# Attention scores of four heads on four groups of 32 partitions, in three passes, with one key tile to a step

## The chip, the cores and the metric

The kernel runs on one core of a Trainium2 chip. The metric is the device time of one execution in microseconds (us); times of the engines come from one profiled execution. TensorE (PE in the profile, its weight loads apart as PEld) multiplies into PSUM, which has eight banks of 128 partitions by 512 fp32 values here; ScalarE (ACT) computes the exponentials, VectorE (DVE) and GpSimd (POOL) do the rest of the arithmetic, SyncE (SP) issues the DMAs.

## What is computed

Two layers, each an attention block and a feed-forward block with residuals, on 2048 tokens of width 448. Attention has 16 query heads of width 28 and one shared key and value head.

```python
q = (x @ wq).reshape(B, S, H, Dh).transpose(0, 2, 1, 3)      # H = 16, Dh = 28
k = x @ wk; v = x @ wv
scores = einsum("bhqd,bkd->bhqk", q, k) * (Dh ** -0.5)
p = softmax(scores, axis=-1)
o = einsum("bhqk,bkd->bhqd", p, v)
x = x + o.transpose(0, 2, 1, 3).reshape(B, S, H * Dh) @ wo    # x was layer-normed on the way in
x = x + (silu(x @ w_gate) * (x @ w_up)) @ w_down              # the same
```

Inputs and output are fp32. Products are made of rounded operands: an fp32 value is split into a high part and a low rest (both fp32r), and a product is high·high + high·low + low·high.

## The kernel before, in words

Work runs in phases on one core: the projections of layer 0 (`project`, `q`, L436 to L495), attention of layer 0 (`scores`, L516), its feed-forward block with the projections of layer 1 at its end (`rest`, L814), attention and feed-forward block of layer 1. A schedule written out by hand fixes the order on each engine: what the Python code issues first stands first in that engine's queue, and a queue is worked off in order. A second, slower form of everything (`full=True`, L58) stands behind a branch that these inputs don't take; in the trace there are 2048 score matmuls, which is one pass over both layers.

**Operands of the scores.** `kstack` (`kt_`, L149) holds the transposed keys four times over in 128 partitions: high part in rows 0 to 27, low part in rows 32 to 59, both again in rows 64 to 91 and 96 to 123. `qstack` (`qts`, L151) holds a head's queries in the same rows as high, high, low, low. One matmul that contracts over all 128 partitions thus makes all four products (the low·low one too) in a single pass. Rows 28 and 92 carry a shift of the exponent (the negated rough maximum, in two parts) against a row of ones in `kstack`. Three `qstack` buffers rotate over the 16 groups (`GR`: a block of 512 queries by four heads). `stack` (L340) loads them from DRAM by four DMAs, `high` (L352) loads a second copy of the high parts (`qhigh`), which the rough maximum uses (`quick_steps`, L363): two matmuls against a block-diagonal tile `kdiag`, a maximum on VectorE, and small DMAs that write the rows.

**The attention loop** (L625). For every group `i` and every two key tiles `k2` (128 keys each), `cycle` (L556) makes eight score tiles of 128 keys by 512 queries: four heads by two key tiles. They go into three PSUM pairs of two banks (`pairs`, banks 0 to 5) and into bank 7 (`one`), which is used twice in a cycle, for the first and the last tile. ScalarE takes each pair in one instruction and each single bank in one (`exps`, L549, line L552 in the profile): five instructions, in the order one, pair, pair, one, pair. The first tile of the next cycle has bank 7 free again while ScalarE still works on the last pair. Behind the eight score matmuls stand the products with the values of the cycle before (`pv`, L576): four heads side by side on four groups of 32 columns, accumulated over the 16 key tiles in bank 6. Before the scores of a cycle stands what is slipped in (L561 to L565): the rough maximum (in two cycles of eight), or an output projection (`outproj`, L532, 12 matmuls; 12 times a layer). In group 6 four transposes of the next block's input (`flip`, L244) go in. They borrow the pair that is free at that time. `post` (L587) copies bank 6 out after each group, and normalises it through DRAM.

**The feed-forward block** works with two matmuls of 64 partitions side by side (`side_by_side`, L290, line L295). It needs the upper rows of one input block a second time (`xd`); before, this copy lies in `qstack2` (L748 and L817), which is cleared again for layer 1 (L839).

Of the kernel before, what the change touches and what calls it, by code (L numbers as in the profile page):

```python
# [29 lines left out]
PB = 6  # L30
# [32 lines left out]
def forward(  # L63
# [30 lines left out]
    phase, banks, pairs, live, turn = ExitStack(), [], [], set(), {}  # L94
    LOW, HIGH, ALL = (0, 1, 2, 3), (4, 5, 6, 7), (4, 5, 6, 7, 0, 1, 2, 3)

    def phases():

        n = 0
        while True:  # L100
            for paired in (False, True):
# [3 lines left out]
                if paired:  # L105
                    pairs[:] = [pool.tile([P, 2, 512], F32, name=f"pair{i}") for i in range(3)]
                    banks[:] = [None] * 6 + kept
                else:
                    pairs[:] = []
                    banks[:] = [pool.tile([P, 512], F32, name=f"bank{i}") for i in range(6)] + kept  # L110
                yield
# [194 lines left out]
    class Attention:  # L306
# [33 lines left out]
        def stack(self, i):  # L340
            c, g = GR[i]
            q = qts[i % 3]
            if full:
                for r in (28, 92):
                    dma(q[r : r + 1, :, :], q[r + 1 : r + 2, :, :])
            for b in range(4):
                src = self.qd[c][b // 2, 112 * g : 112 * g + 112, :]
                nc.sync.dma_start(
                    q[32 * b : 32 * b + DH, :, :].bitcast(F32), src.rearrange("(j d) t -> d j t", d=DH)
                )  # L350

        def high(self, i):  # L352

            c, g = GR[i]
            for j in range(4):
                r = 112 * g + DH * j
                nc.sync.dma_start(qms[i % 2][32 * j : 32 * j + DH, :].bitcast(F32), self.qd[c][0, r : r + DH, :])

        def diagonal(self):
            for j in range(4):  # L360
                dma(kd[32 * j : 32 * j + DH, j, :], kt_[0:DH, 0:64])

        def quick_steps(self, i):  # L363
# [4 lines left out]
            def one(t):  # L368
                if t % 2 == 0:
# [3 lines left out]
                    got["pm"][:, 256 * h : 256 * h + 256], qms[i % 2][:, P * t : P * t + P],  # L373
# [11 lines left out]
            def rows():  # L385
                q = qts[i % 3]
                ng = ngs[i % 2]
                two = pers.tile([P, 32], F32R, name="two")
                nc.vector.tensor_copy(two[:, 0:16], ng)
                nc.vector.tensor_tensor(two[:, 16:32], ng, two[:, 0:16], ALU.subtract)  # L390
                flat = pers.tile([P, 32], F32, name="flat")
                nc.vector.transpose(flat, two.bitcast(F32))
                down = pers.tile([P, 32], F32R, name="down")
                nc.vector.tensor_copy(down, flat)
                for b in range(4):
                    to = q[28:93:64, :, :].rearrange("o j (t w) -> o (j t) w", w=P)
                    dma(to[:, :, 32 * b : 32 * b + 32], down[32 * b : 32 * b + 32, :])
# [3 lines left out]
        def max_steps(self, i):  # L401
# [4 lines left out]
            def one(j, qt, kc):  # L406
# [4 lines left out]
                nc.tensor.matmul(pm, q[:, j, P * qt : P * qt + P], kt_[:, ks], start=True, stop=True)  # L411
# [6 lines left out]
            def place(pn=None):  # L418
# [8 lines left out]
                dma(q[28:29, :, :], nh)  # L427
                dma(q[92:93, :, :], nl)
# [7 lines left out]
        def project(self):  # L436
# [14 lines left out]
            if c == 0 and m < 2:  # L451
                if not full:
                    self.waiting.append(lambda: self.high(m))
                self.waiting.append(lambda: self.stack(m))
# [5 lines left out]
        def q(self, c, m):  # L460
# [23 lines left out]
            for z in range(2):  # L484
                for r in (32 * z, 64 + 32 * z):
                    dma(kt_[r : r + DH, cs], two[96 : 96 + DH, z, :])
# [29 lines left out]
        def scores(self, ff):  # L516
            next(switch)
            with tc.tile_pool(name=f"at{self.layer}", bufs=1) as wp:
# [3 lines left out]
                todo, late, due = [], [], {}  # L522
# [20 lines left out]
                def scores(i, which, sp):  # L543
                    for e, (kt, j) in enumerate(which):
                        nc.tensor.matmul(  # L545
                            sp[:, e, :], kt_[:, P * kt : P * kt + P], qts[i % 3][:, j, :], start=True, stop=True
                        )

                def exps(i, which, sp):  # L549
                    two = len(which) == 2  # L550
                    pt = wp.tile([P, 1 + two, 512], F32, name="pt" if two else "pt1", bufs=PB if two else 4)
                    nc.scalar.activation(pt[:, 0 : len(which), :], sp[:, 0 : len(which), :], AF.Exp, scale=SCALE)  # L552
                    for e, w in enumerate(which):
                        pts[i, w] = pt[:, e, :]

                def cycle(i, k2):  # L556


                    a, b, c = (pairs[(8 * i + k2 + n) % 3] for n in range(3))
                    one = banks[7][:, None, :]  # L560
                    self.lent = a[:, 0, :]  # L561
                    if todo and k2 in (0, 5, 6, 7):
                        todo.pop(0)(a[:, 0, :])
                    if full or k2 in (3, 4):
                        self.advance(2 * KC if full else 2)  # L565
                    ks = [(2 * k2 + n // 4, n % 4) for n in range(8)]
# [7 lines left out]
                    return b  # L574

                def pv(i, kt):  # L576
                    if kt == 0:
                        accs[i] = banks[6]
                    for j in range(4):
                        nc.tensor.matmul(  # L580
                            accs[i][32 * j : 32 * j + 32, :], vsb[:, kt, :], pts.pop((i, (kt, j))),
                            start=(kt == 0), stop=(kt == NT - 1), skip_group_check=True,
                        )
                    if kt == NT - 1:
                        due[8 * i + 9] = post(i)
# [39 lines left out]
                for i in range(len(GR)):  # L625
                    for k2 in range(NT // 2):
                        if k2 == 2 and i + 2 < len(GR):
                            self.stack(i + 2)
                        if k2 == 5 and i + 2 < len(GR) and not full:
                            self.high(i + 2)  # L630
                        if i in (2, 3) and k2 == 4:
                            load_wo(i - 2)
                        if k2 == 4 and 10 < i <= 11 + FG:
                            ff.W[i - 11] = weights(i - 11)

                        free = cycle(i, k2)
                        if k2 == 5 and i + 1 < len(GR) and full:
                            self.places[i + 1](free[:, 0, :])
                        if i == 6 and 0 < k2 < 5:
                            flip(got, X0, [k2 - 1], free[:, 0, :])  # L640
                        while late:
                            pv(*late.pop(0))
                        late += [(i, 2 * k2), (i, 2 * k2 + 1)]
                        if 8 * i + k2 in due:
                            due.pop(8 * i + k2)()
                        if i in (5, 9, 14) and k2 > 2:
                            for f in {5: fs, 9: fs1, 14: ff.second[0][:5]}[i][2 * k2 - 6 : 2 * k2 - 4]:
                                f()
                while late:
                    pv(*late.pop(0))  # L650
# [15 lines left out]
    class FeedForward:  # L666
# [147 lines left out]
        def rest(self, xb):  # L814
            self.xbp = xb.enter_context(tc.tile_pool(name=f"xb{self.layer + 1}", bufs=3))
            self.stage = xb.enter_context(tc.tile_pool(name=f"stage{self.layer}", bufs=2))
            dma(qts[2][64:128, 0, :], self.X[0][0][0:64, 3, :])  # L817
            self.X[0] = (*self.X[0][:2], qts[2][:, 0, :])
# [19 lines left out]
            if self.nxt:  # L838
                nc.gpsimd.memset(qts[2].bitcast(F32), 0.0)  # L839
# [21 lines left out]
    nc.gpsimd.memset(kt_.bitcast(F32), 0.0)  # L861
    ones = halves("ones")[0:1, 0, 0:P]
    nc.gpsimd.memset(ones.bitcast(F32), 1.0)
    for r in (28, 92):
        dma(kt_[r : r + 1, :].rearrange("p (a b) -> p a b", b=P), ones[:, None, :].to_broadcast([1, NT, P]))
    nc.gpsimd.memset(vsb, 0.0)
    nc.gpsimd.memset(vsb[:, :, DH : DH + 1], 1.0)
    for t in [*qms, *([kd] if kd is not None else []), *qts]:
# [42 lines left out]
```

## Time and profile before

| | before |
|---|---|
| time, median of 3 runs | 2081.48 us (2077.92 to 2081.76) |
| profiled execution, its time | 2082.3 us |
| its span | 2080.4 us |
| mean granted clock of TensorE | 0.994 |
| VectorE busy | 513.0 us (25%) |
| GpSimd busy | 497.2 us (24%) |
| TensorE weight loads busy | 1445.6 us (69%) |

In the profile's group lines stand line, engine, operation, output and inputs, shapes, the count, then busy time in us and the mean of one in ns, then the idle time before them and what ended it. A timeline line has the start in us from the beginning of the span, the length in us, the engine, line, operation, and how many instructions of the kind were merged into it; a bracket gives the idle time of the engine before it and who ended it. A matmul's length runs to its modelled end, while the next starts earlier: 0.39 us long, but spaced by less.

### The profile page before, as it was taken

Reading aid. Unit: us, or ns where it says so; the run is one execution under the profiler, and the core shown is the slowest. Engines: PE = TensorE matmul, PEld = TensorE weight load, DVE = VectorE, ACT = ScalarE, POOL = GpSimd, SP = SyncE. Lnnn points to the kernel's source line nnn. Section 1 sums busy time; section 2 is a strip of 40 time slices with the busy share of each in tenths; the row PEclk is TensorE's granted clock in tenths of the full one; section 3 lists DMA queues with packets and bytes.
Section 4 is the critical chain, followed back from the end, with each engine's and each line's share of the span. In section 5 each row is a group of like instructions: output and inputs, shape, how many; then the busy total and the mean of one; then the engine's idle time right before and its main releaser. Section 6 shows DMA issues by size and latency. Waiting matters only on the chain.

```text
span 2080.4 us, 36295 instructions
## 1 busy us (share of the span) xinstructions
PE 2042.6 (98%) x14577; PEld 1445.6 (69%) x14577; DVE 513.0 (25%) x1038; ACT 1317.3 (63%) x2382; POOL 497.2 (24%) x499
## 2 busy tenths in 40 slices
PE   6999999999999999999999999999999999999998
PEld 5544544545548999999875445455454589999997
DVE  6111121211104233222550112212111142323322
ACT  2699799798983333333337997988979733333332
POOL 5202011103112333333341111011122023333321
PEclk9999999999999999999999999999999999999999
DMA  6412122123200111000143222121322001111102
GB/s 182 141 40 61 36 50 51 34 51 64 49 7 23 30 30 30 24 22 25 33 116 95 60 51 46 29 56 29 71 43 48 22 8 30 30 30 30 31 2 73
DMA packets 98738, 98.02 MB, mean 47 GB/s; under 512 B 29024, under 2 KB 68352, under 8 KB 98560
## 3 DMA queue, kind: packets, MB, share of 16 engines
q1 hardware_dynamic: 98560, 95.60, 18.7%
q8 instruction: 117, 1.92, 0.4%
q14 instruction: 61, 0.50, 0.1%
HBM read 73.53 MB, written 18.61 MB: 44 GB/s over the span
## 4 chain that ended last, share of the span: by engine, by line
PE 91%; DMA 3%; DVE 2%; SPq 1%; POOL 1%; ACT 1%; issue 0%; DVEq 0%; ACTq 0%; POOLq 0%
PE bank L295 37%; PE bank L580 21%; PE pair L545 16%; PE bank L545 7%; PE bank L273 3%; PE pair L537 3%; DMA o<-rd 2%; PE pair L372 1%; PE bank L537 1%; PE bank L250 1%; DVE stats L219 0%; DMA qd<-q 0%; SPq L595 0%; DVE xn L232 0%; DMA rs<-o 0%
## 5 line engine op out<-in xcount | busy, mean ns | idle before, releaser
L552 ACT ACTIVATE pt<-pair 128x1024 f32<-128x1024 f32 x768 | 764.4, 1030 | 0.8 <-PE pair L545 0.6
L580 PE MATMUL bank<-pt,vsb 128*32 128x512 f32 x4096 | 492.1, 598 | 0.0
L295 PE MATMUL bank<-xh,wgh 64*128 64x512 f32 x1728 | 460.7, 388 | 0.5
L545 PE MATMUL pair<-qstack,kstack 128*128 128x512 f32 x1536 | 399.9, 395 | 0.9 <-ACT q L476 0.9
L295 PE MATMUL bank<-xh,wgl 64*128 64x512 f32 x1404 | 376.1, 386 | 0.0
L552 ACT ACTIVATE pt<-bank 128x512 f32<-128x512 f32 x512 | 308.4, 602 | 90.2 <-PE bank L545 83.8
L295 PE MATMUL bank<-xl,wgh 64*128 64x512 f32 x1296 | 344.1, 387 | 0.0
L295 PE MATMUL bank<-wdh,h 64*128 64x448 f32 x1792 | 339.7, 366 | 1.2 <-ACT h L794 0.8
L545 PEld LDWEIGHTS pair<-qstack,kstack 128*128 128x128 f32 x1536 | 286.6, 188 | 61.7 <-ACT q L476 1.8
L295 PEld LDWEIGHTS bank<-xh,wgh 64*128 64x128 f32 x1728 | 280.2, 184 | 8.5 <-DVE xl L254 1.6
L580 PEld LDWEIGHTS bank<-pt,vsb 128*32 128x32 f32 x4096 | 107.5, 109 | 244.8 <-issue 243.7
L295 PEld LDWEIGHTS bank<-wdh,h 64*128 64x128 f32 x1792 | 256.7, 185 | 8.5 <-issue 2.5
L613 POOL TENSOR_TENSOR o<-o 128x512 f32<-128x512 f32 x32 | 41.1, 1285 | 892.8 <-DMA o<-rd 557.0
L712 POOL TENSOR_TENSOR xres<-stage,xres 128x448 f32<-128x448 f32 x112 | 131.4, 1195 | 488.1 <-ACT stage L711 488.1
L295 PEld LDWEIGHTS bank<-xh,wgl 64*128 64x128 f32 x1404 | 230.0, 184 | 3.7
L302 ACT COPY seen<-bank 128x1 f32<-128x1 f32 x664 | 82.7, 164 | 236.2 <-PE bank L295 234.4
L295 PE MATMUL bank<-wdl,h 64*128 64x448 f32 x896 | 222.5, 360 | 0.0
L545 PE MATMUL bank<-qstack,kstack 128*128 128x512 f32 x512 | 219.0, 428 | 2.7 <-ACT pt L552 2.7
L295 PEld LDWEIGHTS bank<-xl,wgh 64*128 64x128 f32 x1296 | 209.9, 185 | 2.6
L792 ACT ACTIVATE sg<-bank 128x512 f32<-128x512 f32 x112 | 67.1, 599 | 220.1 <-PE bank L295 210.4
L545 PEld LDWEIGHTS bank<-qstack,kstack 128*128 128x128 f32 x512 | 96.1, 188 | 155.9 <-ACT pt L552 144.3
L793 DVE TENSOR_TENSOR sg<-bank,sg 128x512 f32<-128x512 f32 x112 | 77.5, 692 | 491.9 <-ACT sg L792 482.9
(115 smaller groups left out, 1776.3 us busy)
## 6 DMA issues: line engine op xcount, KB each, us to landing
qstack<-qd SPq DMA_DIRECT2D x128, 224.0 KB
qd<-q SPq DMA_DIRECT2D x24, 512.0 KB
o<-rd SPq DMA_DIRECT2D x32, 256.0 KB
qhigh<-qd SPq DMA_DIRECT2D x128, 56.0 KB
wdr<-in_B_w_down_dram SPq DMA_DIRECT2D x28, 224.0 KB
wr<-in_B_w_gate_dram SPq DMA_DIRECT2D x28, 192.0 KB
wr<-in_B_w_up_dram SPq DMA_DIRECT2D x28, 192.0 KB
out_dram<-xres SPq DMA_DIRECT2D x16, 224.0 KB
```

The lines of the kernel that those rows point to most:

```text
L250: nc.tensor.transpose(pt[:, P * t : P * t + P], got["x"][:, t, P * k : P * k + P], ident)
L273: nc.tensor.matmul(po, a, b, start=(i == 0), stop=(i == len(seq) - 1))
L295: nc.tensor.matmul(po, a, b, start=start, stop=stop, skip_group_check=True)
L302: nc.scalar.copy(seen[:, i : i + 1], po[:, 0:1])
L537: nc.tensor.matmul(po[:, 0:D], a[:, g, ts_], b[:, g, :], start=(g + z == 0), stop=(g == NG - 1 and z == 2))
L545: nc.tensor.matmul(sp[:, e, :], kt_[:, P * kt : P * kt + P], qts[i % 3][:, j, :], start=True, stop=True)
L552: nc.scalar.activation(pt[:, 0 : len(which), :], sp[:, 0 : len(which), :], AF.Exp, scale=SCALE)
L580: nc.tensor.matmul(accs[i][32 * j : 32 * j + 32, :], vsb[:, kt, :], pts.pop((i, (kt, j))), start=(kt == 0), stop=(kt == NT - 1), skip_grou ...
L613: nc.gpsimd.tensor_tensor(rb, oraw, rb, ALU.mult)
L712: nc.gpsimd.tensor_tensor(r, s, r, ALU.add)
L792: nc.scalar.activation(sg, pg[0], AF.Silu)
L793: nc.vector.tensor_tensor(sg, pg[1], sg, ALU.mult)
```

## The change

Each of the four heads of a group gets 32 partitions of its own. `keys` holds high and low part of the keys side by side in the free dimension, repeated in four groups of 32 partitions; `qstack` holds head `j` in partitions 32j to 32j+27, high and low part side by side. A score tile is now made in three passes over 32 partitions (high·high, low key·high query, high key·low query), with the weights at `tile_position=(32*j, 0)`, and the four heads' passes stand one behind the other in the queue: pass 0 of heads 0 to 3, pass 1 of heads 0 to 3, pass 2 of heads 0 to 3. Each head has a PSUM bank of its own.

A step is one key tile (512 steps in all) in place of two. Heads 0 to 2 go into a tile of three banks (two such tiles, which take turns), head 3 into bank 7 in every step. ScalarE takes the three banks in one instruction of 128x1536 and bank 7 in a second one, in that order. The products with the values are those of two steps earlier. What is slipped in stands behind the scores of a step and ahead of these products, in the three banks that are free at that time.

Beside it: `qhigh` and `high` go (the rough maximum reads the high part from `qstack`), `stack` keeps four DMAs in another shape, `kdiag` is filled by GpSimd in place of DMAs, `keys` is preset to ones and zeros in place of two DMAs of a row of ones, and the feed-forward block gets tiles `xd` of its own, so that `qstack2` isn't cleared again.

```diff
-    kt_ = pers.tile([P, S], F32R, name="kstack")
+    keys = pers.tile([P, 2, S], F32R, name="keys")
+    kh, kl = keys[:, 0, :], keys[:, 1, :]
-    qts = [pers.tile([P, 4, 512], F32R, name=f"qstack{n}") for n in range(3)]
-    qms = [pers.tile([P, 512], F32R, name=f"qhigh{n}") for n in range(2)] if not full else []
+    qts = [pers.tile([P, 2, 512], F32R, name=f"qstack{n}") for n in range(3)]
...
-                    pairs[:] = [pool.tile([P, 2, 512], F32, name=f"pair{i}") for i in range(3)]
+                    threes[:] = [pool.tile([P, 3, 512], F32, name=f"three{i}") for i in range(2)]
...
         def stack(self, i):
-            for b in range(4):
-                src = self.qd[c][b // 2, 112 * g : 112 * g + 112, :]
-                nc.sync.dma_start(
-                    q[32 * b : 32 * b + DH, :, :].bitcast(F32), src.rearrange("(j d) t -> d j t", d=DH)
-                )
-        def high(self, i):
...
+                nc.sync.dma_start(
+                    q[32 * j : 32 * j + DH, :, :].bitcast(F32),
+                    self.qd[c][:, r : r + DH, :].rearrange("z d t -> d z t"),
+                )
         def diagonal(self):
             for j in range(4):
-                dma(kd[32 * j : 32 * j + DH, j, :], kt_[0:DH, 0:64])
+                nc.gpsimd.tensor_copy(kd[32 * j : 32 * j + DH, j, :], kh[32 * j : 32 * j + DH, 0:64])
...
-                def cycle(i, k2):
-                    a, b, c = (pairs[(8 * i + k2 + n) % 3] for n in range(3))
-                    one = banks[7][:, None, :]
...
-                    for where, which in ((one, ks[0:1]), (b, ks[1:3]), (c, ks[3:5])):
-                        scores(i, which, where)
-                        exps(i, which, where)
-                    scores(i, ks[5:7], a)
-                    scores(i, ks[7:8], one)
-                    exps(i, ks[7:8], one)
-                    exps(i, ks[5:7], a)
+                def step(n):
+                    i, kt = divmod(n, NT)
+                    three, one = threes[n % 2], banks[7]
+                    q, ks = qts[i % 3], slice(P * kt, P * kt + P)
+                    for z, (k, part) in enumerate(((kh, 0), (kl, 0), (kh, 1))):
+                        for j in range(4):
+                            js = slice(32 * j, 32 * j + 32)
+                            nc.tensor.matmul(
+                                three[:, j, :] if j < 3 else one, k[js, ks], q[js, part, :],
+                                start=(z == 0), stop=(z == 2), tile_position=(32 * j, 0),
+                            )
+                    pt = wp.tile([P, 3, 512], F32, name="pt", bufs=4)
+                    pt1 = wp.tile([P, 512], F32, name="pt1", bufs=4)
+                    nc.scalar.activation(pt, three, AF.Exp, scale=SCALE)
+                    nc.scalar.activation(pt1, one, AF.Exp, scale=SCALE)
+                    pts[n] = [*(pt[:, j, :] for j in range(3)), pt1]
+                def between_steps(n):
+                    i, kt = divmod(n, NT)
+                    free = threes[(n + 1) % 2]
+                    self.lent = free[:, 0, :]
+                    if full or kt in (6, 8):
+                        self.advance(KC if full else 2)
...
+                    if todo and kt in (0, 10, 12, 14):
+                        todo.pop(0)(free[:, 1, :])
+                    if i == 6 and kt in (2, 4, 6, 8):
+                        flip(got, X0, [kt // 2 - 1], free[:, 2, :])
...
+                for n in range(last):
+                    i, kt = divmod(n, NT)
+                    if kt == 4 and i + 2 < len(GR):
+                        self.stack(i + 2)
...
+                    step(n)
+                    between_steps(n)
+                    if n > 1:
+                        pv(n - 2)
+                    if n in due:
+                        due.pop(n)()
...
-                self.X[c] = xtile(self.xbp, qts[2][:, c, :])
+                self.X[c] = xtile(self.xbp, self.xd[c])
...
-            if self.nxt:
-                nc.gpsimd.memset(qts[2].bitcast(F32), 0.0)
...
-    nc.gpsimd.memset(kt_.bitcast(F32), 0.0)
+    nc.gpsimd.memset(kh.bitcast(F32), 1.0)
+    nc.gpsimd.memset(kl.bitcast(F32), 0.0)
```

More of the change, by code (lines that the diff above doesn't have):

```diff
@@ L28 @@
 SCALE = DH ** -0.5
-PB = 6
 LEAD = 4
@@ L93, in forward @@
     kept = [ps.tile([P, 512], F32, name=f"bank{n}") for n in (6, 7)]
-    phase, banks, pairs, live, turn = ExitStack(), [], [], set(), {}
+    phase, banks, threes, live, turn = ExitStack(), [], [], set(), {}
     LOW, HIGH, ALL = (0, 1, 2, 3), (4, 5, 6, 7), (4, 5, 6, 7, 0, 1, 2, 3)
@@ L100, in phases @@
         while True:
-            for paired in (False, True):
+            for wide in (False, True):
                 n += 1
@@ L387, in rows @@
                 ng = ngs[i % 2]
-                two = pers.tile([P, 32], F32R, name="two")
-                nc.vector.tensor_copy(two[:, 0:16], ng)
-                nc.vector.tensor_tensor(two[:, 16:32], ng, two[:, 0:16], ALU.subtract)
+                two = pers.tile([P, 4, 2, 4], F32R, name="two")
+                parts, whole = [two[:, :, z, :] for z in range(2)], ng.rearrange("p (j t) -> p j t", t=4)
+                nc.vector.tensor_copy(parts[0], whole)
+                nc.vector.tensor_tensor(parts[1], whole, parts[0], ALU.subtract)
                 flat = pers.tile([P, 32], F32, name="flat")
-                nc.vector.transpose(flat, two.bitcast(F32))
+                nc.vector.transpose(flat, two.rearrange("p j z t -> p (j z t)").bitcast(F32))
                 down = pers.tile([P, 32], F32R, name="down")
@@ L410, in one @@
                 pm, ks = self.mbank()[1], slice(512 * kc, 512 * kc + 512)
-                nc.tensor.matmul(pm, q[:, j, P * qt : P * qt + P], kt_[:, ks], start=True, stop=True)
+                js, qs = slice(32 * j, 32 * j + 32), slice(P * qt, P * qt + P)
+                for n_, (z, k) in enumerate(((0, kh), (1, kh), (0, kl))):
+                    nc.tensor.matmul(
+                        pm, q[js, z, qs], k[js, ks], start=(n_ == 0), stop=(n_ == 2), tile_position=(32 * j, 0)
+                    )
                 nc.vector.tensor_reduce(got["mx"][:, n, kc : kc + 1], pm, AX.X, ALU.max)
@@ L483, in q @@
                 return
-            for z in range(2):
-                for r in (32 * z, 64 + 32 * z):
-                    dma(kt_[r : r + DH, cs], two[96 : 96 + DH, z, :])
+            for j in range(4):
+                dma(keys[32 * j : 32 * j + DH, :, cs], two[96 : 96 + DH, :, :])
             vt = pers.tile([P, 512], F32, name="sg")[64:96, :]
@@ L521, in scores @@
                 on, accs, pts = {}, {}, {}
-                todo, late, due = [], [], {}
+                todo, due = [], {}
                 def load_wo(z):
@@ L541, in outproj @@
                         nc.vector.tensor_tensor(xres[:, 4 * c + t, :], po[:, 0:D], xres[:, 4 * c + t, :], ALU.add)
[L543 to L554, printed above, removed]
@@ L577, in pv @@
+                def pv(n):
+                    i, kt = divmod(n, NT)
                     if kt == 0:
@@ L624, in scores @@
                 ff.second = norm_steps(2)
[L625 to L650, printed above, removed]
+                last = NT * len(GR)
+                for n in range(last):
+                    i, kt = divmod(n, NT)
+                    if kt == 4 and i + 2 < len(GR):
+                        self.stack(i + 2)
+                    if i in (2, 3) and kt == 8:
+                        load_wo(i - 2)
+                    if kt == 8 and 10 < i <= 11 + FG:
+                        ff.W[i - 11] = weights(i - 11)
+                    step(n)
[4 more added lines that the diff above has]
+                        due.pop(n)()
+                    if i in (5, 9, 14) and kt > 5:
+                        for f in {5: fs, 9: fs1, 14: ff.second[0][:5]}[i][kt - 6 : kt - 5]:
+                            f()
+                for n in (last - 2, last - 1):
+                    pv(n)
                 self.lent = None
@@ L815, in rest @@
             self.xbp = xb.enter_context(tc.tile_pool(name=f"xb{self.layer + 1}", bufs=3))
-            self.stage = xb.enter_context(tc.tile_pool(name=f"stage{self.layer}", bufs=2))
-            dma(qts[2][64:128, 0, :], self.X[0][0][0:64, 3, :])
-            self.X[0] = (*self.X[0][:2], qts[2][:, 0, :])
+            self.stage = xb.enter_context(tc.tile_pool(name=f"stage{self.layer}", bufs=1 if full else 2))
+            xd = xb.enter_context(tc.tile_pool(name=f"xd{self.layer}", bufs=1))
+            self.xd = [xd.tile([P, 512], F32R, name=f"xd{c}") for c in range(NC)]
+            dma(self.xd[0][64:128, :], self.X[0][0][0:64, 3, :])
+            self.X[0] = (*self.X[0][:2], self.xd[0])
             self.turned(1)
@@ L860, in forward @@
     at.turned(0)
-    nc.gpsimd.memset(kt_.bitcast(F32), 0.0)
[L862 to L865, printed above, removed]
+    nc.gpsimd.memset(kh.bitcast(F32), 1.0)
+    nc.gpsimd.memset(kl.bitcast(F32), 0.0)
     nc.gpsimd.memset(vsb, 0.0)
     nc.gpsimd.memset(vsb[:, :, DH : DH + 1], 1.0)
-    for t in [*qms, *([kd] if kd is not None else []), *qts]:
+    for t in [*([kd] if kd is not None else []), *qts]:
         nc.gpsimd.memset(t.bitcast(F32), 0.0)
```

37 lines of the change are left out of this document (15 added, 22 removed).

## The prediction

> **What bounds the kernel now.** I read the page's totals and its chain first, then busy times by stretch, then the timeline of one undisturbed cycle.
>
> ```profile
> span 2080.4 us, 36295 instructions
> PE 2042.6 (98%) x14577; PEld 1445.6 (69%) x14577; DVE 513.0 (25%) x1038; ACT 1317.3 (63%) x2382; POOL 497.2 (24%) x499
> PE 91%; DMA 3%; DVE 2%; SPq 1%; POOL 1%; ACT 1%; issue 0%; DVEq 0%; ACTq 0%; POOLq 0%
> ```
>
> ```profile
> 75.98:614.96 538.98, 536.69 (x3265) 269.70 (x3267) 81.78 (x232) 493.53 (x639) 80.28 (x80) 1.00 0.22 48
> 1104.20:1643.79 539.59, 536.89 (x3265) 269.62 (x3267) 82.54 (x232) 493.60 (x639) 80.31 (x80) 1.00 0.22 48
> sum 1078.57, PE 1073.58 PEld 539.32 DVE 164.32 ACT 987.12 POOL 160.59; mean PE 536.79 PEld 269.66 DVE 82.16 ACT 493.56 POOL 80.29
> ```
>
> The two stretches run from the first to the last score matmul of each layer's attention: 1078.6 us, which is all that the change rewrites. TensorE is busy through it and carries the chain, but ScalarE is busy for 987 us of it (92%): two engines stand close together there, and what one waits for the other soon matters.
>
> ```profile
> 404.89 0.50 PE L545 MATMUL bank<-qstack,kstack 128*128 128x512 f32 x1
> 405.22 1.56 PE L545 MATMUL pair<-qstack,kstack 128*128 128x512 f32 x6
> 406.62 0.39 PE L545 MATMUL bank<-qstack,kstack 128*128 128x512 f32 x1
> 406.94 1.92 PE L580 MATMUL bank<-pt,vsb 128*32 128x512 f32 x16
> 408.79 0.50 PE L545 MATMUL bank<-qstack,kstack 128*128 128x512 f32 x1
> ```
>
> ```profile
> 405.94 1.94 ACT L552 ACTIVATE pt<-pair 128x1024 f32<-128x1024 f32 x2
> 407.77 0.61 ACT L552 ACTIVATE pt<-bank 128x512 f32<-128x512 f32 x1
> 408.24 1.05 ACT L552 ACTIVATE pt<-pair 128x1024 f32<-128x1024 f32 x1
> ```
>
> A bare cycle of two key tiles lasts 408.79 − 404.89 = 3.90 us on TensorE. The six matmuls from 405.22 and the seventh at 406.62 are spaced by 0.23; a change between the two shapes of matmul costs some 0.1 more (406.62 to 406.94 is 0.32). The products with the values take 408.79 − 406.94 = 1.85 for two key tiles. ScalarE's pairs are spaced by (407.77 − 405.94) / 2 = 0.915, a single bank by 408.24 − 407.77 = 0.47: 3 × 0.915 + 2 × 0.47 = 3.69 of the 3.90. Of 1078.6 us, 256 × 3.90 = 998 are bare cycles; the other 80 is what is slipped in.
>
> **What the change makes of a step.** By throughput alone it looks good. On ScalarE a step would need the three banks, 0.915 for two of them and for the third what one bank more costs, and the single one at 0.47.
>
> ```profile
> L552 ACT ACTIVATE pt<-pair 128x1024 f32<-128x1024 f32 x768 | 764.4, 1030 | 0.8 <-PE pair L545 0.6
> L552 ACT ACTIVATE pt<-bank 128x512 f32<-128x512 f32 x512 | 308.4, 602 | 90.2 <-PE bank L545 83.8
> ```
>
> A bank more is 1.030 − 0.602 = 0.43, so the three banks take 1.345 until the next instruction starts, and the step 1.345 + 0.47 = 1.81, against 3.69 / 2 = 1.845 before. (The form of 128x1536 isn't in this trace. Three single banks would be 3 × 0.47 = 1.41, one and a half pairs 1.37; I keep 1.345, the row's own slope.)
>
> But the queue has a wait in each step that can't hide. Head 3 has bank 7 alone. Its pass 0 of step n+1 must wait until ScalarE has read bank 7 of step n, and that is the last thing ScalarE does in step n. Behind the waiting matmul in TensorE's queue stand the passes 1 and 2 of all heads, the products with the values and everything later; ScalarE's next instruction, the three banks of step n+1, waits for pass 2 of head 2. So in each step ScalarE stands still while TensorE makes two passes. Before, ScalarE still has a pair queued when bank 7 is asked for; only the very first cycle, without the products in between, shows the same pattern:
>
> ```profile
> 79.41 0.60 ACT L552 ACTIVATE pt<-bank 128x512 f32<-128x512 f32 x1
> ...
> 78.32 0.39 PE L545 MATMUL bank<-qstack,kstack 128*128 128x512 f32 x1
> 80.06 0.50 PE L545 MATMUL bank<-qstack,kstack 128*128 128x512 f32 x1 [1.35 <-ACT pt L552]
> 80.40 1.77 PE L545 MATMUL pair<-qstack,kstack 128*128 128x512 f32 x6
> ...
> 80.06 0.19 PEld L545 LDWEIGHTS bank<-qstack,kstack 128*128 128x128 f32 x1 [1.79 <-ACT pt L552]
> 80.17 0.19 PEld L545 LDWEIGHTS pair<-qstack,kstack 128*128 128x128 f32 x1
> ```
>
> Bank 7 is done at 79.41 + 0.60 = 80.01; the weight load, which carries the wait too, starts at 80.06: 0.05 from ScalarE to TensorE. The matmul is 0.50 long rather than 0.39, as its weights weren't loaded ahead (0.11, the spacing of the loads at 80.06 and 80.17).
>
> What follows a release with several groups of partitions is shown by the feed-forward block, which runs two of 64 side by side; here the upper one waited:
>
> ```profile
> 661.16 0.86 PE L295 MATMUL bank<-xh,wgh 64*128 64x512 f32 x2
> 661.53 0.18 PEld L295 LDWEIGHTS bank<-xh,wgh 64*128 64x128 f32 x1 [0.38 <-DVE sg L793]
> 661.54 0.29 PEld L295 LDWEIGHTS bank<-xl,wgh 64*128 64x128 f32 x2
> 661.54 0.72 PE L295 MATMUL bank<-xl,wgh 64*128 64x512 f32 x2
> 661.64 0.41 PEld L295 LDWEIGHTS bank<-xh,wgl 64*128 64x128 f32 x2
> 661.88 0.40 PE L295 MATMUL bank<-xh,wgl 64*128 64x512 f32 x1
> 662.12 0.60 PE L295 MATMUL bank<-xh,wgh 64*128 64x512 f32 x2
> ```
>
> Three things are to be seen. The lower half's next load (661.54), which waits for nothing of its own, came only with the released one: a blocked head of the queue holds the other groups as well. Loads of the two groups then start within 0.01 of each other, so they overlap. And the next round of matmuls starts at 661.88, 0.34 after the release, the one after at 662.12, 0.24 later. I take the same for four groups of 32: with the release of bank 7, head 3's pass 0 and the others' pass 1 start together; 0.34 later, behind head 3's pass 1, pass 2 of heads 0 to 2; it is 0.40 long (the matmul at 661.88). That is 0.74 from release to the end of pass 2.
>
> (The Trainium skill, TensorE: Matmul & The Clock Gate, Part 3, gives 3.07 times the speed for four row tiles of 32, where four would be perfect; this trace has no four. By it, as an estimate, a round of four would take 4 × 0.23 / 3.07 = 0.30, and as one round lies on the path, the step would be 0.07 longer and the whole 36 us, which the range holds.)
>
> Last, from TensorE to ScalarE:
>
> ```profile
> 405.42 0.60 ACT L552 ACTIVATE pt<-bank 128x512 f32<-128x512 f32 x1
> 405.45 0.40 PE L545 MATMUL pair<-qstack,kstack 128*128 128x512 f32 x1
> ```
>
> The matmul at 404.89 ends at 405.39 and ScalarE starts at 405.42: 0.03. The one at 405.45 completes a pair at 405.85 and its exponential starts at 405.94: 0.09. The new wide instruction carries the same two waits as that pair, so I take 0.10.
>
> The step: 1.345 (three banks) + 0.60 (bank 7, to its end) + 0.05 + 0.74 + 0.10 = **2.84 us**, against 1.95 before. 512 × 2.84 = 1454 us.
>
> TensorE's own work fits inside, which is why its gain is worth nothing: three rounds at 0.34, 0.23 and 0.32 and half of 1.85 for the products, with one more change of shape, 0.05, make 1.87 of 2.84.
>
> **What is slipped in.** The rough maximum (two matmuls, 0.5 us) now falls into this idle second: free. An output projection doesn't fit:
>
> ```profile
> 230.21 0.47 PE L537 MATMUL pair<-woh,onh 128*128 128x448 f32 x1
> ...
> 232.75 0.40 PE L545 MATMUL bank<-qstack,kstack 128*128 128x512 f32 x1
> ...
> 288.49 0.69 DVE L253 CAST xh<-pair 128x512 fp32r<-128x512 f32 x1 [1.87 <-PE pair L250]
> 289.21 0.69 DVE L254 TENSOR_TENSOR xl<-pair,xh 128x512 fp32r<-128x512 f32 x1
> ```
>
> Its 12 matmuls take 232.75 − 230.21 = 2.54. From a release: the third round starts at 0.34 + 0.23 = 0.57, the projection at 0.90, it ends at 3.44, the products (0.1 + 0.93 + 0.05) at 4.5; then all three rounds of the next step follow, one more than after a wait. The step is 4.5 − 2.84 + 0.23 = 1.9 longer, times 24 is 45 us. The eight transposed blocks hold a bank for VectorE's two instructions (0.69 each) and cost some 0.5 each: 5 us with two that meet a rough maximum. First and last step of each layer: 5 us. Attention: 1454 + 45 + 5 + 5 = 1509.
>
> **The rest** I cost at nothing, with ±10 us for it: fewer and shorter DMAs for the queries, one clearing of a buffer less, GpSimd copies for `kdiag`. They stand beside the projections, where TensorE is the bound as the chain has it; DMA is 3% of that chain. If the cover is gone, a query load that comes late costs a few us once a group, but each is issued 28 steps ahead. SyncE's queue holds nothing new in front of it.
>
> **Sum.** The profiled execution took 2082.3 us (span 2080.4), 0.8 above the median of 2081.48. 2082.3 + 1509 − 1078.6 = 2512.7; against the median 2512.
>
> **Rivals.**
>
> *The other heads pass the blocked one (faster).* If TensorE let heads 0 to 2 make their passes while head 3 waits for bank 7, the three banks would be ready when ScalarE ends the step, and the bound would be TensorE's 1.87: 512 × 1.87 + 80 = 1037, a gain of 41 us, **2040**. It decides as soon as pass 2 of head 2 can end ahead of bank 7's release. For it: the groups are independent, and TensorE has a second to spare. Against: rows 661.16 to 661.54, where the free half stood still for 0.37. (The Trainium skill, same page and part, says that weight loads may be pulled ahead for another row group but that matmuls start and end in their order; by that rule this rival falls, and the trace agrees.)
>
> *Weight loads one after the other.* Twelve loads a step rather than four. If four groups don't load at once, eight stand between the release and pass 2 of head 2: the last begins at 7 × 0.11 = 0.77, then 0.11 and 0.40, 1.28 rather than 0.74: 512 × 0.54 = 276, **2790**. Against it: the two loads at 661.53 and 661.54; four are not shown.
>
> *No side by side at all*, the change not doing what it says: eight matmuls behind the release, 0.34 + 6 × 0.23 + 0.40 = 2.12 rather than 0.74: 512 × 1.38 = 707, **3220**. Against it: the same rows, and the four column groups of L580, 16 of which take 1.92.
>
> *A slower clock.* TensorE would idle for about 0.9 us in each step; the granted clock is 1.00 in both stretches now. At half of it 0.74 would be 1.4: some 340 us more, **2850**.
>
> **Chances.** Forecast 0.80, the faster rival 0.05, serial loads 0.06, no overlap 0.05, clock 0.02; 0.02 for smaller gains that I don't see. The forecast's own bounds: 0.03 to 0.10 into ScalarE (−36), three banks at 1.33 to 1.41 (−8 to +33), the round (+36), the rest ±10, projections ±15: 2440 to 2600, which serves as the range, since the other cases hold 2 in 10. Faster by over 0.2% (about what a measurement tells here) 0.06, within it 0.01, slower 0.93.
>
> **What would show it.** In the attention stretches ScalarE's wide instruction should show about 0.9 us idle ahead of it, ended by a score matmul, 500 times, some 450 us in all; TensorE's first load of bank 7 should be ended by ScalarE's single exponential each step; steps spaced by 2.84; the stretches about 1509 us. Wide instructions with no idle time and bank 7 without a wait would make me wrong; rounds spaced by more than 0.4 would name the second or third rival, a clock below 1.00 the last.

## The result, and the profile after

| | before | changed |
|---|---|---|
| median | 2080.28 us (4 runs, 2077.92 to 2081.76) | 2497.32 us (4 runs, 2496.78 to 2499.42) |
| ratio | | 1.2008, 95% interval 1.1987 to 1.2029 |
| span of the profiled execution | 2080.4 us | 2495.9 us |
| attention stretches | 1078.6 us | 1507.8 us |
| outside of them | 1001.8 us | 988.1 us |

The change makes the kernel 20% slower; 2512 us were forecast, 2440 to 2600 as the range. The page of the changed kernel, and the two stretches from the first to the last score matmul of each layer:

```profile
span 2495.9 us, 44645 instructions
PE 2257.7 (90%) x18673; PEld 1392.6 (56%) x18673; DVE 516.6 (21%) x1038; ACT 1315.6 (53%) x2126; POOL 494.2 (20%) x504
PE 60%; issue 22%; ACT 14%; DVE 2%; SPq 1%; DMA 1%; POOL 0%; ACTq 0%; DVEq 0%
...
L552 ACT ACTIVATE pt<-three 128x1536 f32<-128x1536 f32 x512 | 742.6, 1450 | 515.7 <-PE three L546 444.7
L546 PE MATMUL bank<-qstack,keys 32*128 32x512 f32 x1536 | 495.5, 428 | 199.7 <-ACT pt L553 198.5
```

```profile
70.10:824.50 754.40, 649.08 (x5321) 246.34 (x5324) 81.88 (x232) 495.00 (x512) 80.00 (x80) 1.00 0.09 22
1306.40:2059.80 753.40, 649.56 (x5321) 246.54 (x5324) 86.49 (x232) 495.10 (x512) 79.87 (x80) 1.00 0.09 22
sum 1507.80, PE 1298.64 PEld 492.88 DVE 168.38 ACT 990.11 POOL 159.87; mean PE 649.32 PEld 246.44 DVE 84.19 ACT 495.05 POOL 79.94
```

ScalarE does as much as before in attention (990 us busy, 987 before), but in 1508 us instead of 1079: 66% rather than 92%. Ahead of its wide exponential it stood idle for 515.7 us in all, 444.7 of them ended by a score matmul, and the score matmuls into bank 7 waited 198.5 us for `pt L553`, the exponential of bank 7. Each engine waits for the other in turn. That TensorE is "busy" for 90% of the span says little: each matmul counts to its modelled end. The timeline of one step, ScalarE, TensorE, and the weight loads around the release:

```profile
402.21 0.59 ACT L553 ACTIVATE pt<-bank 128x512 f32<-128x512 f32 x1
403.71 1.45 ACT L552 ACTIVATE pt<-three 128x1536 f32<-128x1536 f32 x1 [0.90 <-PE three L546]
405.06 0.59 ACT L553 ACTIVATE pt<-bank 128x512 f32<-128x512 f32 x1
```

```profile
402.86 0.49 PE L546 MATMUL bank<-qstack,keys 32*128 32x512 f32 x1 [0.50 <-ACT pt L553]
402.86 0.50 PE L546 MATMUL three<-qstack,keys 32*128 32x512 f32 x3
403.19 0.39 PE L546 MATMUL bank<-qstack,keys 32*128 32x512 f32 x1
403.20 0.39 PE L546 MATMUL three<-qstack,keys 32*128 32x512 f32 x3
403.43 0.39 PE L546 MATMUL bank<-qstack,keys 32*128 32x512 f32 x1
403.75 1.07 PE L575 MATMUL bank<-pt,vsb 128*32 128x512 f32 x8
404.75 0.51 PE L546 MATMUL three<-qstack,keys 32*128 32x512 f32 x3
405.70 0.50 PE L546 MATMUL bank<-qstack,keys 32*128 32x512 f32 x1 [0.45 <-ACT pt L553]
```

```profile
402.86 0.18 PEld L546 LDWEIGHTS bank<-qstack,keys 32*128 32x128 f32 x1 [0.82 <-ACT pt L553]
402.86 0.19 PEld L546 LDWEIGHTS three<-qstack,keys 32*128 32x128 f32 x3
```

Bank 7 is read until 402.21 + 0.59 = 402.80. At 402.86 head 3's pass 0 starts, and the other three heads' pass 1 with it. At 403.20 the three make pass 2, which ends at 403.59; ScalarE's wide instruction starts at 403.71, after 0.90 us of idling. Pass 0 of the next step's heads 0 to 2 starts at 404.75, long before head 3 gets bank 7 again at 405.70: 2.84 us after the last time.

### The profile page after: what moved, and what is told of

The parts are those of the page before. It is cut to its first block, busy times and chain, and to the rows that moved or that the text cites. A ratio compares the mean times of both kernels' runs of the same rounds, so it can differ in the third digit from the quotient of the medians.

```text
span 2495.9 us, 44645 instructions
## 1 busy us (share of the span) xinstructions
PE 2257.7 (90%) x18673; PEld 1392.6 (56%) x18673; DVE 516.6 (21%) x1038; ACT 1315.6 (53%) x2126; POOL 494.2 (20%) x504
## 4 chain that ended last, share of the span: by engine, by line
PE 60%; issue 22%; ACT 14%; DVE 2%; SPq 1%; DMA 1%; POOL 0%; ACTq 0%; DVEq 0%
PE bank L294 31%; PE bank L546 12%; ACT pt L553 10%; PE three L546 6%; PE bank L575 3%; ACT pt L552 3%; PE three L532 3%; PE bank L272 2%; PE three L365 1%; PE bank L532 1%; PE bank L249 1%; DVE xl L253 0%; SPq L131 0%; DMA qd<-q 0%; DVE stats L218 0%
## 5 line engine op out<-in xcount | busy, mean ns | idle before, releaser
L552 ACT ACTIVATE pt<-three 128x1536 f32<-128x1536 f32 x512 | 742.6, 1450 | 515.7 <-PE three L546 444.7
L546 PE MATMUL bank<-qstack,keys 32*128 32x512 f32 x1536 | 495.5, 428 | 199.7 <-ACT pt L553 198.5
L546 PE MATMUL three<-qstack,keys 32*128 32x512 f32 x4608 | 625.3, 459 | 5.8 <-DVE xl L253 3.4
L575 PE MATMUL bank<-pt,vsb 128*32 128x512 f32 x4096 | 546.8, 606 | 0.0
L546 PEld LDWEIGHTS three<-qstack,keys 32*128 32x128 f32 x4608 | 250.8, 183 | 435.2 <-issue 352.8
L546 PEld LDWEIGHTS bank<-qstack,keys 32*128 32x128 f32 x1536 | 244.8, 184 | 369.6 <-ACT pt L553 350.0
L294 PE MATMUL bank<-xh,wgh 64*128 64x512 f32 x1728 | 427.1, 388 | 0.5
L553 ACT ACTIVATE pt<-bank 128x512 f32<-128x512 f32 x512 | 303.1, 592 | 0.0
L294 PEld LDWEIGHTS bank<-xh,wgh 64*128 64x128 f32 x1728 | 246.4, 184 | 8.6 <-DVE xl L253 1.6
L294 PEld LDWEIGHTS bank<-xl,wgh 64*128 64x128 f32 x1296 | 184.4, 184 | 2.9
L575 PEld LDWEIGHTS bank<-pt,vsb 128*32 128x32 f32 x4096 | 81.3, 108 | 173.2 <-issue 163.3
```

Source lines behind the costliest of these rows:

```text
L294: nc.tensor.matmul(po, a, b, start=start, stop=stop, skip_group_check=True)
L546: nc.tensor.matmul(three[:, j, :] if j < 3 else one, k[js, ks], q[js, part, :], start=(z == 0), stop=(z == 2), tile_position=(32 * j, 0),)
L552: nc.scalar.activation(pt, three, AF.Exp, scale=SCALE)
L553: nc.scalar.activation(pt1, one, AF.Exp, scale=SCALE)
L575: nc.tensor.matmul(accs[i][32 * j : 32 * j + 32, :], vsb[:, kt, :], pts[n][j], start=(kt == 0), stop=(kt == NT - 1), skip_group_check=True,)
```

## Experiments

Theory: head 3's bank is asked for in the middle of TensorE's queue and released as the last thing in ScalarE's, and whatever stands behind the blocked matmul stands still with it. Main rival: twelve small matmuls with twelve weight loads in place of four large ones, with changes of shape in every step, are too much for TensorE. Single profiled runs have no interval of their own. In the swaps and with fewer passes the differences are far above the spread of a few us that the timed kernels show; outside attention they are not, and there the spread is told with them.

### The order on ScalarE alone

```diff
-                    nc.scalar.activation(pt, three, AF.Exp, scale=SCALE)
                     nc.scalar.activation(pt1, one, AF.Exp, scale=SCALE)
+                    nc.scalar.activation(pt, three, AF.Exp, scale=SCALE)
```

> The changed kernel with ScalarE's two exponentials of a step in the other order: bank 7 first, the three banks second. All twelve score matmuls, all weight loads and the order on TensorE stay. Theory (the wait for bank 7, asked for first and released last, costs ScalarE two rounds in every step): bank 7 is free 0.6 us after the scores are done, long before TensorE asks for it, so the step falls from 2.85 us to what TensorE needs by itself, about 1.87 (ScalarE needs 1.81); with some 80 us of slipped-in work per run the attention stretches fall from 1508 to about 1040 us and the kernel to about 2030 (2010 to 2070), faster than the kernel before. Rival (twelve small matmuls and weight loads in place of four, or changes of shape twice as often, are what costs): the order on ScalarE changes nothing, about 2497.

Measured: 2089.65 us (5 runs), 1.0037 times the kernel before (1.0022 to 1.0051). Two swapped lines take away 408 of the 417 us. No matmul was changed, so the rival falls. The wait for bank 7 is gone, 0.3 us where it was 199.7:

```profile
L546 PE MATMUL bank<-qstack,keys 32*128 32x512 f32 x1536 | 491.7, 425 | 0.3 <-ACT pt L552 0.3
```

But it isn't the 2030 that I expected. One bare step on TensorE:

```profile
301.32 0.50 PE L546 MATMUL three<-qstack,keys 32*128 32x512 f32 x3
...
303.22 0.50 PE L546 MATMUL three<-qstack,keys 32*128 32x512 f32 x3
```

The step is 303.22 − 301.32 = 1.90 rather than 1.87, 15 us over 512 (a key tile took 3.90 / 2 = 1.95 before). The rest is slipped-in work: the stretches take 1099.3 us, so 1099.3 − 512 × 1.90 = 126 us of it, where the 80 of the kernel before was expected. A step with a rough maximum shows about half of these 46 us:

```profile
207.74 0.51 PE L546 MATMUL three<-qstack,keys 32*128 32x512 f32 x3
...
208.91 0.51 PE L365 MATMUL three<-kdiag,qstack 128*128 128x256 f32 x2 [0.21 <-ACT pt L553]
209.35 1.06 PE L575 MATMUL bank<-pt,vsb 128*32 128x512 f32 x8
210.34 0.50 PE L546 MATMUL three<-qstack,keys 32*128 32x512 f32 x3
```

It takes 210.34 − 207.74 = 2.60, 0.70 more than a bare step (`L553` is the wide exponential in this kernel). The two matmuls borrow the three banks that ScalarE now reads last, and wait 0.21 for them; they also stand between two other shapes. The kernel before had three pairs, one was free by then, and the same two matmuls (`L372` there) wait for nothing:

```profile
211.15 0.50 PE L545 MATMUL bank<-qstack,kstack 128*128 128x512 f32 x1
...
215.06 0.50 PE L372 MATMUL pair<-kdiag,qhigh 128*128 128x256 f32 x2
...
219.55 0.39 PE L545 MATMUL bank<-qstack,kstack 128*128 128x512 f32 x1
```

Two cycles with a rough maximum last 219.55 − 211.15 = 8.40 there, two bare ones 7.80: 0.30 for each. 60 steps have one, so 60 × 0.40 = 24 us of the 46. By medians over the same two traces an output projection costs 2.93 in place of 2.45 (24 of them, 12 us), and the eight steps with transposes cost 9 us more.

In attention the new layout thus stays 1099.3 − 1078.6 = 20.7 us longer than the old one even with the order swapped. That the whole kernel comes within 0.4% is due to the time outside attention, 988.5 us against 1001.8.

### Fewer passes

The third pass left out (no product of high key and low query), and then the second as well (no product with a low part):

```diff
-                    for z, (k, part) in enumerate(((kh, 0), (kl, 0), (kh, 1))):
+                    for z, (k, part) in enumerate(((kh, 0), (kl, 0))):
...
```

> The changed kernel without the third pass (high key times low query is left out, so its scores lack that product). Theory of the wait: one round fewer lies between the release of bank 7 and the end of the three banks, so the step loses one round, 0.235 us: 2.61 us, about 2375 in all. Rival of TensorE's throughput: 1.9 of the 2.85 us belong to twelve score matmuls, eight cost a third less, so the step loses about 0.6: about 2180.

Measured: 2380.5 us. ScalarE's timeline:

```profile
400.30 1.45 ACT L552 ACTIVATE pt<-three 128x1536 f32<-128x1536 f32 x1 [0.61 <-PE three L546]
...
402.91 1.45 ACT L552 ACTIVATE pt<-three 128x1536 f32<-128x1536 f32 x1 [0.67 <-PE three L546]
```

The step is 2.61 and the idle time 0.67 in place of 0.90: a third of the score matmuls gone, and the step is one round shorter, no more. That is the wait's arithmetic and not that of throughput.

> The changed kernel with the first pass alone (high times high; both products with a low part are left out). Theory of the wait: heads 0 to 2 need no matmul behind the blocked one any more, the three banks are ready before bank 7 is released, and the wait vanishes from ScalarE's path: the step falls to ScalarE's own 1.82 us, a second drop of about 0.8 us after one of 0.235, in all about 1980. Rival of throughput: the second pass left out gives as much as the first, about 0.6 us again or less.

Measured: 2122.57 us, not 1980. The three banks are indeed ready without the blocked matmul, but something is left:

```profile
329.79 1.46 ACT L552 ACTIVATE pt<-three 128x1536 f32<-128x1536 f32 x1
331.14 0.60 ACT L553 ACTIVATE pt<-bank 128x512 f32<-128x512 f32 x1
331.37 0.50 PE L546 MATMUL three<-qstack,keys 32*128 32x512 f32 x3
331.79 0.49 PE L546 MATMUL bank<-qstack,keys 32*128 32x512 f32 x1
331.98 1.45 ACT L552 ACTIVATE pt<-three 128x1536 f32<-128x1536 f32 x1 [0.24 <-PE three L546]
332.21 1.07 PE L575 MATMUL bank<-pt,vsb 128*32 128x512 f32 x8
333.20 0.50 PE L546 MATMUL three<-qstack,keys 32*128 32x512 f32 x3
333.81 1.45 ACT L552 ACTIVATE pt<-three 128x1536 f32<-128x1536 f32 x1
```

Steps are 2.19 and 1.83 in turn. The matmul that waits for bank 7 (331.79, after 331.14 + 0.60) also holds back the products with the values (332.21) and, through them, the next three heads (333.20). I had followed the queue behind the blocked matmul only to the next exponential. The second pass left out gave 2.61 to about 2.0, more than the 0.24 of the first one, as the wait has it and as a cost per matmul has not; its size was 0.2 too large. That is 0.19 × 512 = 97 of the 143 us over 1980; the rest is slipped-in work that costs more than I assumed.

### The same wait in the kernel before

```diff
-                    exps(i, ks[7:8], one)
                     exps(i, ks[5:7], a)
+                    exps(i, ks[7:8], one)
```

> The kernel before, with one swap: in each cycle the last pair is exponentiated ahead of the second use of bank 7, so that bank 7 is released last there too. No passes, no new shapes, all else as before. Theory of the wait: ScalarE loses about 0.7 us in each cycle of two key tiles; a cycle goes from 3.90 to about 4.46 us, 143 us over 256 cycles, less some 30 for slipped-in work that now falls into idle time: 2190 to 2225. Rival (the three passes cost the time, not the order): about 2080 as before.

Measured: 2185.05 us. A cycle on TensorE and ScalarE:

```profile
133.56 0.51 PE L545 MATMUL bank<-qstack,kstack 128*128 128x512 f32 x1 [0.48 <-ACT pt L552]
...
138.02 0.50 PE L545 MATMUL bank<-qstack,kstack 128*128 128x512 f32 x1 [0.48 <-ACT pt L552]
```

```profile
134.62 2.85 ACT L552 ACTIVATE pt<-pair 128x1024 f32<-128x1024 f32 x3
137.35 0.62 ACT L552 ACTIVATE pt<-bank 128x512 f32<-128x512 f32 x1
138.55 0.60 ACT L552 ACTIVATE pt<-bank 128x512 f32<-128x512 f32 x1 [0.58 <-PE bank L545]
```

138.02 − 133.56 = 4.46, as worked out. So some 105 us come from one swapped line with none of the new layout in it. That the total is 5 us under the expected range is mostly the slipped-in work: the two stretches grew by 1184.7 − 1078.6 = 106 us, so 37 us of it, and not 30, fell into the idle time; the time outside attention came out 3 us shorter in this trace. The wait alone is shown, in both kernels and both ways.

### The 13.7 us outside attention

The changed kernel gains 5.9 us ahead of layer 0's scores and 7.3 between the layers' scores, which I had costed at nothing. Five kernels ask where from:

```diff
-                nc.gpsimd.tensor_copy(kd[32 * j : 32 * j + DH, j, :], kh[32 * j : 32 * j + DH, 0:64])
+                dma(kd[32 * j : 32 * j + DH, j, :], kh[0:DH, 0:64])
```

> The changed kernel, but the block-diagonal tile of keys is filled by four DMAs from the first keys again, as in the kernel before, rather than by GpSimd. It asks where the 13.7 us come from that the changed kernel gains outside the attention stretches (5.9 us ahead of the first scores, 7.3 us from the end of layer 0's scores to the start of layer 1's). Theory of the query loads (in the projections SyncE's queue has the four loads of the second query copy less to issue, and the other loads stand one projection earlier, so the stores of the projected queries land sooner and their buffers come free sooner): no difference here, the stretches outside attention stay at 988 us. Rival (the DMAs of the diagonal wait for the keys and hold SyncE's queue): about 6 us of loss in each layer, 1000 us outside attention.

Measured: 2496.7 us, with 988.7 us outside attention (its span of 2494.8 less two stretches that add up to 1506.1). No difference in the sum.

```diff
...
+                if not full:
+                    self.waiting.append(lambda: self.high(m))
                 self.waiting.append(lambda: self.stack(m))
```

> The changed kernel with the loads of the second query copy put back during the projections alone (two groups a layer, four DMAs each, in the old places of the queue, into a scratch buffer in DRAM that nothing reads). Theory of the query loads: the gain outside attention goes, 988 us back to about 1000. Rival of the diagonal: 988 us as it is.

Measured: 2505.05 us. Outside attention, ahead of, between and behind the stretches:

```profile
0.00:73.30 73.30, 55.30 (x244) 42.97 (x244) 39.77 (x81) 20.28 (x35) 38.26 (x67) 0.98 0.64 189
828.60:1313.60 485.00, 479.49 (x4021) 447.65 (x4020) 173.67 (x285) 162.08 (x551) 167.27 (x166) 1.00 0.14 40
2067.40:2503.30 435.90, 426.33 (x3777) 410.35 (x3777) 135.34 (x208) 143.76 (x518) 129.29 (x113) 0.99 0.10 30
```

994.2 us: 3.2 more ahead of the scores (73.3 against 70.1) and 3.1 between them (485.0 against 481.9). How much of that is spread is seen in the other kernels of this document whose projections are those of the changed kernel (the exponentials swapped, two passes, one pass, the diagonal by DMA, the buffer cleared): 68.1 to 69.9 us ahead, 481.8 to 484.3 between, 987.4 to 989.2 in all. The kernel before with its exponentials swapped has 75.1, 486.8 and 998.5, where the kernel before has 76.0, 489.2 and 1001.8. So 5 to 7 us in all come back, of a gain of 10 to 14: about half of it was this load. Ahead of the scores that is clear; between the layers 485.0 lies too near to 484.3 to tell. The remainder was sought in the clearing of the third query buffer:

> The changed kernel with the clearing of the third query buffer between the layers put back on GpSimd (now half the size, about 1 us). The second query copy explained 8 of the 13.7 us gained outside attention, 5 of 6 ahead of layer 0 but 3 of 7 between the layers; this asks whether the clearing holds the other 4 there. If it stands in front of GpSimd's share of the projections: 1 to 4 us more between the layers, 2498 to 2501. If not: 2497, and the rest belongs to the shorter loads (the four loads of a group carry half the bytes).

Measured: 2497.82 us, nothing. (The split of "8 of 13.7" in that text was taken from the totals; by the stretches it is 6.) No part of the rest is seen in the clearing, though the spread between the layers would hide an effect of up to 2 us. From the other side, the kernel before with the load of group 1's queries moved behind the projections:

```diff
-                self.waiting.append(lambda: self.stack(m))
+                if full or m == 0:
+                    self.waiting.append(lambda: self.stack(m))
...
+                        if i == k2 == 0 and not full:
+                            self.stack(1)
```

> The kernel before with one load moved: the queries of group 1 are loaded at the start of the attention loop rather than during the projections (they are needed 16 key tiles later). Theory of the query loads: the 3 us that SyncE spends on them no longer stand ahead of the stores of projected queries, and most of the 6 us a layer comes off: 2080 to about 2070 (2067 to 2075). Rival (the order of SyncE's queue isn't what delays, or the diagonal is): about 2080.

Measured: 2072.97 us, 0.9963 times the kernel before (0.9950 to 0.9977), with 992.0 us outside attention in place of 1001.8. That load's four issues stand in SyncE's queue ahead of the stores of projected queries, in the kernel before (here ahead of layer 1):

```profile
1077.89 3.10 SPq L348 DMA_DIRECT2D qstack<-qd  x4
1081.09 0.38 SPq L479 DMA_DIRECT2D qd<-q  x1
```

and ScalarE waits for those stores before it can fill their buffers anew (longest wait 4.6 us):

```profile
ACT q L476 <- DMA qd<-q: 5.2, 2, 4.6
ACT q L473 <- DMA qd<-q: 4.0, 1, 4.0
```

With the load moved, the same list of waits has (the lines stand one further down)

```profile
ACT q L474 <- DMA qd<-q: 2.6, 1, 2.6
...
ACT q L477 <- DMA qd<-q: 0.7, 1, 0.7
```

The changed kernel has both effects: no second copy, and so the other loads one projection earlier. Which share belongs to the shorter loads wasn't separated. Both loads moved:

> The kernel before with both loads of group 1 (queries and their second copy) moved to the start of the attention loop. The first of them alone gave 2073. Theory of the query loads: with 1.3 us a layer less in SyncE's queue during the projections, 1 to 4 us more come off: 2069 to 2072. If the queue has slack by now: 2073 again; slower than 2073 if the copy now comes late for the rough maximum 6 key tiles later.

Measured: 2071.26 us, 0.9949 (0.9936 to 0.9963), the fastest of all kernels here and, as far as the intervals tell, no faster than with one load moved; outside attention both have 992.0 us. It keeps the old layout of the scores.

## Why the prediction was right, point by point

- **The wait for bank 7** ("the queue has a wait in each step that can't hide"): shown three ways, by the swap in the changed kernel, by the swap in the kernel before, and by the passes left out.
- **The step, 2.84 us**: measured 2.84 to 2.85. Three banks until the next instruction 405.06 − 403.71 = 1.35 (1.345 taken); bank 7 0.59 (0.60); ScalarE to TensorE 0.06 (0.05); release to the end of pass 2 0.73 (0.74); TensorE to ScalarE 0.12 (0.10).
- **Output projections, 1.9 us each**: the wide exponentials are spaced by 4.68 where one was slipped in, 1.83 above a step. The rough maximum is free, as worked out: the step from 278.14 has one, and lasts 2.79.

```profile
278.14 1.45 ACT L552 ACTIVATE pt<-three 128x1536 f32<-128x1536 f32 x1 [0.91 <-PE three L546]
...
278.19 0.51 PE L365 MATMUL three<-kdiag,qstack 128*128 128x256 f32 x2
...
280.93 1.45 ACT L552 ACTIVATE pt<-three 128x1536 f32<-128x1536 f32 x1 [0.85 <-PE three L546]
...
283.78 1.46 ACT L552 ACTIVATE pt<-three 128x1536 f32<-128x1536 f32 x1 [0.91 <-PE three L546]
...
288.46 1.45 ACT L552 ACTIVATE pt<-three 128x1536 f32<-128x1536 f32 x1 [2.75 <-PE bank L546]
```

- **Attention, 1509 us**: 1507.8. That it is so near is in part luck: the eight steps with transposes cost 9 us and not 5 (0.5 each, but 1.8 for the four that meet a rough maximum), while the other 56 steps with a rough maximum were 0.06 shorter than bare ones, 3 us.
- **The rest, nothing ±10**: −13.7 in these two traces, outside its bound. This term failed: I named the projections as the cover ("TensorE is the bound as the chain has it") though the chain of that phase holds waits of ScalarE for stores (4.05 us from 1084.60 in the kernel before), and "SyncE's queue holds nothing new" was true but looked past what leaves that queue. These 13.7 are the difference between 2512 and the measured time, nearly all of it.
- **The other heads pass the blocked one**: no. The weight loads of the three others at 402.86 came with the released one, after 0.82 of idle time, with banks and data ready.
- **Serial loads, no overlap**: no. The four heads' matmuls of a round start within 0.01 of each other and the rounds are 0.33 and 0.24 apart. The Trainium skill's 3.07 (TensorE: Matmul & The Clock Gate, Part 3) would give, as an estimate, 0.30 for the second of these; measured, a round of four costs about what one matmul did (0.23).
- **A slower clock**: no. Both stretches show 1.00, with TensorE idle for about 0.5 us in every step. (The price of this rival was low, too: twice 0.74 is 1.48, not 1.4, so 379 us and 2890.) The Trainium skill (TensorE: Matmul & The Clock Gate, "A second HAM failure mode: psum-queue depth-cycling") tells of a kernel that cycled through PSUM banks and whose short idle pieces made its clock fall again and again; nothing of that is seen here.
- **TensorE's own 1.87**: 1.90 once the wait was gone. What failed there was the expectation of the first experiment that slipped-in work would cost the same as before.

## What to carry to other kernels

When two engines hand buffers back and forth, compare the order in which one asks for them with the order in which the other releases them: the buffer with no second copy has to be released first. In a queue that is worked off in order, count everything behind the blocked instruction, on other partitions too, and follow it past the first consumer. Before a layout is given up or praised, swap the order of the consumers: here two lines decided over 408 us, and the new layout with the better order takes 2% longer than the old one in attention, which a gain elsewhere hides in the total.

## What the runs showed of the hardware beyond that

- A matmul that waits for a semaphore holds matmuls and weight loads of other groups of 32 partitions that wait for nothing (402.86).
- Four groups of 32 partitions with 512 columns each run side by side at nearly the full rate (rounds 0.24 apart; one large matmul before 0.23).
- A bank more in one exponential costs 0.42 to 0.43 us: 0.60, 1.03 and 1.45 us for one, two and three.
